# Spreading the counts of a routing search on VectorE instead of TensorE

## The chip, the cores and the metric

The kernel runs on one core of a Trainium2 chip. The metric is device time in microseconds of one execution, as the median over runs. The core has five engines with a queue of their own each: TensorE (PE in the profile; its weight loads are PEld), VectorE (DVE), ScalarE (ACT), GpSimd (POOL) and SyncE (SP, which only issues DMAs here). An engine works through its queue in the order of the program.

## The reference

Three stages in a row, all in float32:

```
x   = retention(q, k, v)            # 8 batches, 8 heads, 576 positions, 64 wide -> 4608 rows of 512
h   = top1_experts_with_capacity(x) # 8 experts of 512 -> 1024 -> 512, 576 rows each
out = (relu(h w_in) + alpha * min(h w_in, 0)) w_out      # 512 -> 2048 -> 512
```

The middle stage is what the change touches. The reference sorts all 4608 x 8 gate values and gives them out from the highest down: a row goes to the first expert that is offered to it and still has room, and every expert takes exactly 576 rows.

```
for idx in argsort(-logits.flatten()):
    tok, e = idx // 8, idx % 8
    if assigned[tok] < 0 and counts[e] < 576: assigned[tok] = e; counts[e] += 1
```

## The kernel before, in words

Rows lie as 36 chunks of 128 partitions. The attention part fills the gate values `Lg` (128 x 36 x 8). After that the kernel alternates eight experts with eight rounds of the second network: `expert(k)` multiplies the 576 rows of expert k (first layer: 16 groups of 12 matmuls over 288 columns; second layer: 8 groups of 24), `second(y, ...)` takes 512 of the resulting rows through the second network: for each of 16 blocks of the hidden width 12 matmuls `mm` over 512 columns (L969 to L971), clipping on VectorE (L974, L976), a copy on ScalarE (L978) and a subtraction on VectorE (L979) that split the result in two halves `hl`, and 12 matmuls into `acc` (L960), one block later than their `mm`. Left-over columns are gathered in `yl` for a last round.

Which rows expert k takes, and which expert comes next, is not sorted but searched, by `route(k)`. A routing finds, by bisection on the bits of each row's best remaining gate value, the highest value at which some expert becomes full. It runs over `STEPS`: six rounds, each with w thresholds (64, 32, 32, 32, 32, 65). In a round
- VectorE compares all 128 x 36 values with the w thresholds (`compare`, two halves, L425) into G,
- TensorE multiplies G by the one-hot choice O, chunk by chunk, which counts for each expert and threshold how many values lie above (`counts4`, 36 small matmuls in four row groups, L438),
- VectorE adds the four row groups (L517 to L520) and flags, per expert, the thresholds whose count has reached the expert's room R8 (`ind`, L521). These lie on 8 partitions, one for each expert,
- TensorE multiplies `ind` by a matrix of ones (L524), so that each of 128 partitions holds, per threshold, the number of experts that passed, and VectorE counts the thresholds that at least one passed (`n`, L528). From n come the thresholds of the next round (L471).

After six rounds VectorE picks for each expert the counts at the found threshold (`s8`, L535 to L538), puts them on a diagonal `D` (L540), and TensorE multiplies D by ones (L544) so that all partitions have them. VectorE then finds the expert that is full (`t8`) and how many rows with the same value it still needs (`need`, L556 to L563), marks the rows (L570, L573) and makes running counts along the chunks (L576, L578). TensorE multiplies these by two triangles (L583, L584), VectorE makes slot numbers, five small matmuls (L606) put the row numbers in order, GpSimd gathers the rows (L824), and `turn_x` and `place_x` turn and split them for the next expert.

`route(0)` runs ahead of the first expert and isn't part of the change. Routings 1 to 6 (`if k`) run beside the expert and the second network of the one before them. They are a generator: the main stream calls `tick()` at fixed places, each tick lets the routing emit its instructions up to the next `yield`, and so the yields set how far apart a routing's pieces stand in every engine's queue. The order is written out by hand; nothing moves instructions later. From the second expert on, `expert` gives 16 ticks: in the first layer after every second group, in the second layer after every group, each time ahead of the group's ScalarE and VectorE work (L918/L919, L942/L944). For the first expert the ticks of the first layer are listed in `TICKS`, and two more stand in the middle of groups (`MID`). `second` gives a tick after each `mm` block, ahead of its clipping, and one after each `acc` block. What is left of the generator at the end of `second` is emitted there.

A round takes four ticks (comparisons; counts; sums and flags; the matmul with ones), the sixth has one more, and the expert's counts take two.

## Time and profile before

| what | value |
|---|---|
| median of 3 runs | 1501.84 us (1501.71 to 1503.36) |
| profiled execution | 1498.49 us, span 1496.7 us |
| mean granted TensorE clock | 0.986 of full speed |
| TensorE busy (matmul) | 1437.6 us, 96% |
| TensorE weight loads | 1255.3 us, 84% |
| VectorE busy | 926.5 us, 62% |
| ScalarE busy | 396.4 us, 26% |
| GpSimd busy | 179.4 us, 12% |

A row of a group of instructions reads: line, engine, operation, what it writes <- what it reads, shapes, count | busy time in us, mean ns of one | idle time of the engine just ahead of them and what ended it. A matmul's busy time contains its way through the array, and matmuls overlap; the step from one start to the next says what one costs. A row in order of time reads: start, duration in us, then the same names, and in brackets idle time ahead of it with what ended it.

### The profile page before, as it was taken

The numbers are of one execution on the slowest core, as the hardware profiler recorded it, in microseconds if no ns is written. First come the engines' busy times: TensorE is split into PE (matmuls) and PEld (weight loads), VectorE is DVE, ScalarE is ACT, GpSimd is POOL, SyncE is SP. The second block draws the span as 40 slices with busy tenths as digits, with TensorE's granted clock in tenths as the row PEclk, the third lists the DMA queues.
The fourth block names the chain that finished last, engine by engine and source line by source line (L and its number), as shares of the span: only waits on it lengthen the run. The fifth ranks groups of instructions, "written<-read, shape, count | busy, mean of one in ns | idle before, by whom it ended". The sixth has DMA issues, their size and how long they took to land.

```text
span 1496.7 us, 25946 instructions
## 1 busy us (share of the span) xinstructions
PE 1437.6 (96%) x10556; PEld 1255.3 (84%) x10556; DVE 926.5 (62%) x2132; ACT 396.4 (26%) x740; POOL 179.4 (12%) x195
## 2 busy tenths in 40 slices
PE   9899958999999999999999999999999999999997
PEld 8888848978797889788978997898789888988886
DVE  4888878587846675668465856675666435333433
ACT  4566613222421141114111411141124112211111
POOL 3455511001100110011001100110012001000101
PEclk9999978999999999999999999999999999999999
DMA  8999814368734743464457444734576554355652
GB/s 296 361 344 346 312 58 162 127 254 270 222 114 169 246 134 141 169 220 132 141 175 225 133 156 172 221 131 145 193 213 160 191 214 166 107 183 188 219 192 83
DMA packets 97943, 287.57 MB, mean 192 GB/s; under 512 B 45984, under 2 KB 46368, under 8 KB 79392
## 3 DMA queue, kind: packets, MB, share of 16 engines
q1 hardware_dynamic: 78400, 230.12, 46.0%
q10 hardware_dynamic: 13344, 35.87, 6.2%
q0 software_dynamic: 6080, 19.93, 4.2%
q8 instruction: 83, 1.36, 0.4%
q14 instruction: 36, 0.29, 0.1%
HBM read 232.67 MB, written 44.04 MB: 185 GB/s over the span
## 4 chain that ended last, share of the span: by engine, by line
PE 59%; issue 17%; DVE 13%; ACT 7%; DMA 2%; POOL 1%; ACTq 1%; SPq 0%; POOLq 0%
PE acc L960 15%; PE mm L969 6%; PE mm L971 6%; PE mm L970 6%; PE mm L913 4%; PE acc L913 4%; DVE whl L799 3%; PE mm L932 2%; PE acc L932 2%; PE mm L934 2%; PE acc L934 2%; PE acc L933 2%; PE mm L933 2%; ACT whl L798 2%; DVE cv_r L226 2%
## 5 line engine op out<-in xcount | busy, mean ns | idle before, releaser
L960 PE MATMUL acc<-whl,hl 128*128 128x512 f32 x1608 | 388.3, 391 | 0.4 <-ACT hl L978 0.4
L960 PEld LDWEIGHTS acc<-whl,hl 128*128 128x128 f32 x1608 | 299.8, 188 | 65.3 <-issue 2.3
L978 ACT ACTIVATE hl<-tmp 128x512 fp32r<-128x512 f32 x144 | 91.0, 632 | 644.8 <-DVE tmp L976 639.5
L974 DVE TENSOR_SCALAR tmp<-mm,AL 128x512 f32<-128x512 f32 x144 | 107.7, 748 | 185.1 <-PE mm L971 184.6
L969 PE MATMUL mm<-act,whl 128*128 128x512 f32 x512 | 203.1, 397 | 3.8 <-ACT whl L798 2.3
L971 PE MATMUL mm<-act,whl 128*128 128x512 f32 x512 | 200.0, 391 | 0.3 <-DVE whl L799 0.3
L970 PE MATMUL mm<-act,whl 128*128 128x512 f32 x512 | 199.9, 391 | 0.0
L979 DVE TENSOR_TENSOR hl<-tmp,hl 128x512 fp32r<-128x512 f32 x144 | 99.7, 692 | 110.0 <-ACT hl L978 110.0
L824 POOL DMA_INDIRECT rows<-x_rows,gi x40 | 43.1, 1077 | 684.8 <-DVE ec L638 514.6
L969 PEld LDWEIGHTS mm<-act,whl 128*128 128x128 f32 x512 | 96.3, 188 | 24.3 <-ACT whl L798 2.7
L971 PEld LDWEIGHTS mm<-act,whl 128*128 128x128 f32 x512 | 96.5, 188 | 21.3 <-DVE whl L799 1.0
L799 DVE TENSOR_TENSOR whl<-raw,whl 128x1024 fp32r<-128x1024 f32 x80 | 97.8, 1224 | 24.7 <-ACT whl L798 24.4
L970 PEld LDWEIGHTS mm<-act,whl 128*128 128x128 f32 x512 | 96.5, 188 | 19.0
L913 PE MATMUL mm<-act,whl 128*128 128x288 f32 (+2 forms) x768 | 109.8, 299 | 0.7 <-ACT act L854 0.7
L913 PEld LDWEIGHTS mm<-act,whl 128*128 128x128 f32 x768 | 105.8, 192 | 1.8 <-ACT act L854 0.9
L913 PE MATMUL acc<-act,whl 128*128 128x288 f32 (+2 forms) x768 | 107.3, 297 | 0.0
L913 PEld LDWEIGHTS acc<-act,whl 128*128 128x128 f32 x768 | 103.7, 189 | 0.3
L976 DVE SCALAR_TENSOR_TENSOR tmp<-mm,tmp 128x512 f32<-128x512 f32 x144 | 99.6, 692 | 5.0
L798 ACT ACTIVATE whl<-raw 128x1024 fp32r<-128x1024 f32 x80 | 84.0, 1051 | 26.0 <-DVE eqc L642 26.0
L1003 POOL DMA_INDIRECT out<-rows,ix x32 | 34.4, 1076 | 443.4 <-DVE rows L999 438.2
L932 PE MATMUL mm<-act,whl 128*128 128x288 f32 x256 | 76.7, 300 | 0.0
L932 PE MATMUL acc<-act,whl 128*128 128x288 f32 x256 | 76.6, 299 | 0.0
(236 smaller groups left out, 2221.5 us busy)
## 6 DMA issues: line engine op xcount, KB each, us to landing
whl<-w_parts SPq DMA_DIRECT2D x128, 1024.0 KB, 4.8
raw<-in_w SPq DMA_DIRECT2D x64, 512.0 KB, 4.3
a_in<-in_att SPq DMA_DIRECT2D x34, 768.0 KB, 6.8
cv_in<-in_w SPq DMA_DIRECT2D x32, 512.0 KB, 7.8
w_parts<-whl ACTq DMA_DIRECT2D x16, 1024.0 KB, 6.2
x_rows<-xn ACTq DMA_DIRECT2D x36, 256.0 KB, 5.5
w_f<-cv_r ACTq DMA_DIRECT2D x32, 256.0 KB, 7.0
raw<-w_f SPq DMA_DIRECT2D x16, 512.0 KB, 5.8
```

Source lines behind the costliest of these rows:

```text
L798: ACT.activation(w[:, 0], t, AF.Copy)
L799: V.tensor_tensor(w[:, 1], t, w[:, 0].bitcast(F32), op=OP.subtract)
L913: PE.matmul(ps, w[:, wi, wc], x[:, xi, c, hh], start=(wi, xi, c) == (0, 0, 0), stop=(xi, c) == (1, 3))
L932: PE.matmul(ps, w[:, 0, cs], h[:, 0, c % 4, hh], start=c == 0, stop=False)
L960: PE.matmul(acc[tt], hl[:, hi, tt * 128:tt * 128 + 128], w[:, wi, 512:1024], start=f == 0 and (wi, hi) == (0, 0), stop=False)
L969: PE.matmul(ps, w[:, 0, cs], y[:, 0, c, 0:512], start=c == 0, stop=False)
L970: PE.matmul(ps, w[:, 0, cs], y[:, 1, c, 0:512], start=False, stop=False)
L971: PE.matmul(ps, w[:, 1, cs], y[:, 0, c, 0:512], start=False, stop=c == 3)
L974: V.tensor_scalar(t, ps, 0.0, AL[:, f:f + 1], op0=OP.min, op1=OP.mult)
L976: V.scalar_tensor_tensor(g, ps, 0.0, t, op0=OP.max, op1=OP.add)
L978: ACT.activation(hl[:, 0], g, AF.Copy)
L979: V.tensor_tensor(hl[:, 1], g, hl[:, 0].bitcast(F32), op=OP.subtract)
```

## The change

In routings 1 to 6 the two multiplications by ones are gone. `passed` does the first on VectorE: the flags are written to the top 8 rows of a 32-row tile of zeros (`IND[w]`, one for each of the three widths rounded up to 32), turned in blocks of 32 x 32 so that thresholds lie on partitions, the maximum over experts is taken, this is repeated over 32 columns and turned back, which puts all thresholds' answers on each of 32 partitions, and their sum is n. `spread` copies n from partitions 0 to 31 to the other three quarters. After the sixth round the chosen counts `s8`, now in the first rows of a 32-row tile, are turned in the same way (`every`), the small work on them runs on 32 partitions, and `spread` copies its two results. The yields around the removed matmuls are gone, and the first round has one more between its comparisons and its counts. A routing before has 25 yields from the first comparisons to the end of the sixth round's last matmul and two more to the running counts; after, 14 to the same point.

```diff
@@ -353,7 +353,12 @@
     slots2 = keep.tile([128, 2, 640], F16, name="slots2")
     C2 = {}
 
+    IND = {w: keep.tile([32, -(-w // 32) * 32], F32, name=f"ind{w}") for w in sorted({w for _, w in STEPS})}
+    s32 = keep.tile([32, 2], F32, name="s32")
+
     def route_consts():
+        for t in (*IND.values(), s32):
+            V.memset(t, 0.0)
         V.tensor_copy(RT[:, 36:38], CONST["pcol"])
         C2["j01"] = CONST["j01"].rearrange("p (z j) -> p z j", z=2)
         V.memset(Aw, 0.0)
@@ -438,6 +443,25 @@
             PE.matmul(GT["p"][r:r + 8, :w], O[:, c, :], GT["G"][:, c, :w], start=c < 4, stop=c >= NCH - 4,
                       tile_position=(0, r))
 
+    def spread(t):
+
+        for a in (32, 64, 96):
+            V.tensor_copy(t[a:a + 32], t[0:32])
+
+    def passed(ind):
+
+        b = ind.shape[1] // 32
+        turned = rt.tile([32, 3, 32], F32, name="turned")[:, 0:b]
+        flat = turned.rearrange("p a b -> p (a b)")
+        some = rt.tile([32, 3], F32, name="some")[:, 0:b]
+        n = small("n", 1, bufs=2)
+        V.transpose(flat, ind)
+        V.tensor_reduce(some, turned[:, :, 0:8], axis=AX.X, op=OP.max)
+        V.transpose(flat, some.unsqueeze(2).to_broadcast([32, b, 32]))
+        V.tensor_reduce(n[0:32], flat, axis=AX.X, op=OP.add)
+        spread(n)
+        return n
+
     EXP, IDX, GI = {}, {}, {}
 
     def route(k):
@@ -477,7 +501,7 @@
                         compare(key, thr, w, a, b)
                     if k:
                         yield
-                        if s == 5:
+                        if s in (0, 5):
                             yield
                     if k:
                         counts4(w)
@@ -509,7 +533,6 @@
                     u = [ua, ub]
                 yield
                 p = GT["p"]
-                ind = rt.tile([8, 65], BF, name="ind")
                 tot = p[0:8, 0:65]
                 if k:
 
@@ -518,9 +541,11 @@
                     V.tensor_tensor(tot[:, :w], p[64:72, :w], tot[:, :w], op=OP.add)
                     V.tensor_tensor(tot[:, :w], p[96:104, :w], tot[:, :w], op=OP.add)
                     V.tensor_tensor(tot[:, :w], p[0:8, :w], tot[:, :w], op=OP.add)
+                    V.tensor_scalar(IND[w][0:8, :w], tot[:, :w], R8[:, 0:1], None, op0=OP.is_ge)
+                    n = passed(IND[w])
+                    continue
+                ind = rt.tile([8, 65], BF, name="ind")
                 V.tensor_scalar(ind[:, :w], tot[:, :w], R8[:, 0:1], None, op0=OP.is_ge)
-                if k:
-                    yield
                 PE.matmul(p[:, 128:128 + w], ones8, ind[:, :w], start=True, stop=True)
                 yield
                 sj = small("sj", 65)
@@ -528,7 +553,7 @@
                 V.tensor_scalar(sj[:, :w], p[:, 128:128 + w], 0.5, 0.0, op0=OP.is_ge, op1=OP.add, accum_out=n)
 
             j01 = C2["j01"]
-            s8 = rt.tile([8, 2], F32, name="s8")
+            s8 = s32[0:8, :]
             cc = rt.tile([8, 2], F32, name="cc")
             for zi in range(2):
                 scr = rt.tile([8, 65], F32, name="scr", bufs=2)
@@ -536,12 +561,18 @@
                                        op1=OP.mult, accum_out=cc[:, zi:zi + 1])
             V.tensor_tensor(s8[:, 0:1], cc[:, 0:1], R8, op=OP.is_ge)
             V.tensor_tensor(s8[:, 1:2], R8, cc[:, 1:2], op=OP.subtract)
-            D = rt.tile([8, 2, 8], F32, name="D")
-            V.tensor_tensor(D, ident[0:8, None, 0:8].to_broadcast([8, 2, 8]),
-                            s8.unsqueeze(2).to_broadcast([8, 2, 8]), op=OP.mult)
             if k:
-                yield
-            PE.matmul(p[:, 256:272], ones8f, D.rearrange("p a b -> p (a b)"), start=True, stop=True)
+
+                every = rt.tile([32, 2, 32], F32, name="every")
+                V.transpose(every.rearrange("p a b -> p (a b)"), s32.unsqueeze(2).to_broadcast([32, 2, 32]))
+                z0, z1 = every[:, 0, 0:8], every[:, 1, 0:8]
+            else:
+                D = rt.tile([8, 2, 8], F32, name="D")
+                V.tensor_tensor(D, ident[0:8, None, 0:8].to_broadcast([8, 2, 8]),
+                                s8.unsqueeze(2).to_broadcast([8, 2, 8]), op=OP.mult)
+                PE.matmul(p[:, 256:272], ones8f, D.rearrange("p a b -> p (a b)"), start=True, stop=True)
+                z0, z1 = p[:, 256:264], p[:, 264:272]
+            h = z0.shape[0]
             T = small("T", 1)
             V.scalar_tensor_tensor(T, n, 1.0, u[1], op0=OP.mult, op1=OP.add)
             gt = small("gt")
@@ -551,16 +582,19 @@
             gv_ = small("gv_")
             V.tensor_tensor(gv_, gt, vm, op=OP.mult)
             V.tensor_tensor(Aw, Aw, gv_, op=OP.add)
-            yield
-            zc = small("zc", 8)
-            V.scalar_tensor_tensor(zc, p[:, 256:264], -100.0, ecol, op0=OP.mult, op1=OP.add)
-            zm = small("zm", 1)
+            if not k:
+                yield
+            zc = small("zc", 8)[0:h]
+            V.scalar_tensor_tensor(zc, z0, -100.0, ecol[0:h], op0=OP.mult, op1=OP.add)
+            zm = small("zm", 1)[0:h]
             V.tensor_reduce(zm, zc, axis=AX.X, op=OP.min)
-            t8 = small("t8", 1)
-            V.tensor_scalar(t8, zm, -1.0, -92.0, op0=OP.mult, op1=OP.add)
-            nd = small("nd", 8)
-            need = small("need", 1)
-            V.scalar_tensor_tensor(nd, zc, zm, p[:, 264:272], op0=OP.is_equal, op1=OP.mult, accum_out=need)
+            tn = small("tn", 2)
+            t8, need = tn[:, 0:1], tn[:, 1:2]
+            V.tensor_scalar(t8[0:h], zm, -1.0, -92.0, op0=OP.mult, op1=OP.add)
+            nd = small("nd", 8)[0:h]
+            V.scalar_tensor_tensor(nd, zc, zm, z1, op0=OP.is_equal, op1=OP.mult, accum_out=need[0:h])
+            if k:
+                spread(tn)
         ei = small("ei", 1, I32, bufs=2)
         V.tensor_scalar(ei, t8, -1.0, 8.0, op0=OP.mult, op1=OP.add)
         EXP[k] = ei
```

## Rows read from the trace of the kernel before

**Rows 1.** One second network: stretch, length, busy PE, PEld, DVE, ACT, POOL, clock
```profile
447.50:536.00 88.50, 88.50 (x497) 71.22 (x497) 56.09 (x143) 12.88 (x22) 5.45 (x6) 1.00 0.58 189
```

**Rows 2.** Groups of instructions on TensorE, 240 to 1100 us
```profile
L524 PE MATMUL misc<-ind,ones 8*128 8x32 bf16 (+2 forms) x36 | 6.8, 188 | 2.2 <-DVE ind L521 2.2
L544 PE MATMUL misc<-D,ones8f 8*128 8x16 f32 x12 | 2.3, 268 | 0.0
```

**Rows 3.** TensorE in order of time around one spreading matmul
```profile
573.24 0.29 PE L934 MATMUL acc<-act,whl 128*128 128x288 f32 x1
573.46 0.18 PE L524 MATMUL misc<-ind,ones 8*128 8x32 bf16 x1
573.58 0.40 PE L932 MATMUL acc<-act,whl 128*128 128x288 f32 x1
573.81 0.29 PE L933 MATMUL acc<-act,whl 128*128 128x288 f32 x1
573.94 0.30 PE L934 MATMUL acc<-act,whl 128*128 128x288 f32 x1
```

**Rows 4.** Waits of TensorE, 240 to 1100 us: total, times, longest
```profile
PE misc L438 <- DVE G L425: 6.0, 7, 1.1
...
PE misc L524 <- DVE ind L521: 2.2, 1, 2.2
```

**Rows 5.** Granted clock (the number behind POOL) in four stretches
```profile
262.00:265.00 3.00, 3.00 (x15) 2.77 (x13) 1.70 (x7) 0.40 (x2) 0.00 (x0) 0.63 0.55 175
...
326.60:330.00 3.40, 3.40 (x15) 2.74 (x15) 2.35 (x4) 1.58 (x2) 0.00 (x0) 1.00 0.95 345
377.00:381.00 4.00, 1.52 (x5) 0.48 (x3) 2.96 (x4) 1.57 (x2) 0.00 (x0) 0.91 0.92 258
381.00:384.00 3.00, 2.85 (x7) 2.32 (x8) 2.64 (x7) 1.15 (x2) 0.00 (x0) 0.55 0.91 339
```

**Rows 6.** TensorE in order of time, start of a second network
```profile
594.02 0.50 PE L969 MATMUL mm<-act,whl 128*128 128x512 f32 x1
...
599.69 0.18 PE L524 MATMUL misc<-ind,ones 8*128 8x32 bf16 x1
```

**Rows 7.** VectorE in order of time, 576 to 635 us
```profile
576.39 0.19 DVE L471 SCALAR_TENSOR_TENSOR thr<-n,tb 128x32 f32<-128x32 f32 x1
576.61 1.43 DVE L425 TENSOR_TENSOR G<-hf,thr 128x576 bf16<-128x576 f32 x2
...
594.85 0.18 DVE L517 COPY tot<-misc 8x32 f32<-8x32 f32 x1
...
597.08 0.75 DVE L974 TENSOR_SCALAR tmp<-mm,AL 128x512 f32<-128x512 f32 x1 [1.12 <-PE mm L971]
597.86 0.69 DVE L976 SCALAR_TENSOR_TENSOR tmp<-mm,tmp 128x512 f32<-128x512 f32 x1
599.25 0.69 DVE L979 TENSOR_TENSOR hl<-tmp,hl 128x512 fp32r<-128x512 f32 x1 [0.70 <-ACT hl L978]
...
620.58 0.22 DVE L517 COPY tot<-misc 8x65 f32<-8x65 f32 x1
...
621.61 0.25 DVE L521 TENSOR_SCALAR ind<-tot,R 8x65 bf16<-8x65 f32 x1
...
626.53 0.28 DVE L535 SCALAR_TENSOR_TENSOR scr<-tables,n,tot 8x65 f32<-8x65 f32 x1
...
627.24 0.16 DVE L540 TENSOR_TENSOR D<-c_ident,s 8x16 f32<-8x16 f32 x1
...
632.06 0.15 DVE L546 SCALAR_TENSOR_TENSOR T<-n,ub 128x1 f32<-128x1 f32 x1
...
634.00 0.21 DVE L578 TENSOR_TENSOR_SCAN sc<-tables,eqm 128x36 bf16<-128x36 f32 x1
```

**Rows 8.** Groups of instructions on VectorE: one column, and 180 columns
```profile
L508 DVE SCALAR_TENSOR_TENSOR ub<-n,ua 128x1 f32<-128x1 f32 x14 | 2.1, 151 | 0.0
...
L639 DVE TENSOR_REDUCE rf<-ec 128x5 f32<-128x180 f32 x8 | 2.7, 342 | 0.3
```

## The prediction, made blind

> **What bounds the kernel now.** I read the share of busy time by engine first, and then only the stretches that the change touches: the six background routings, 240 to 1100 us. In one whole run of the second network (88.5 us) TensorE is busy all the time, VectorE for 56.1 us of it and ScalarE for 12.9 [rows 1]. The reader should see two things there: whatever TensorE no longer does is time won, and VectorE is free for a third of the time on average, which says nothing yet about a single stretch. The second view was TensorE's groups of instructions: 36 spreading matmuls (six routings of six rounds) and 12 for the chosen expert's counts (six pairs) [rows 2]. Then TensorE in order of time around one of these, its waits, and VectorE in order of time around a routing's end.
>
> **What goes.** A spreading matmul costs more than its 188 ns of busy time suggests. In the first layer the step from the start of the last large matmul to that of the next one, past the small one, is 573.24 to 573.58 = 0.34 us, where an undisturbed step is 0.13; the step after it is 0.23 too [rows 3]. So 0.21 + 0.10 = 0.31 us each, 36 x 0.31 = 11.2 us. The pair for the expert's counts has two matmuls of 268 ns instead of one of 188 [rows 2]; I take 0.5 us for each of six, 3.0 us (between 0.31 and 0.62, one and two such interruptions). Waits go as well: in the stretch TensorE waits 6.0 us for the comparisons and 2.2 us, once, for the flags [rows 4]. The flags' wait goes with its matmul. The comparisons' waits nearly all belong to the first round, whose counts are put off by one more tick, that is by 24 matmuls or 3.1 us, against a longest wait of 1.1 us. Together 8.2 us. Behind the two such waits of the first background routing the granted clock is 0.63 for 3 us [rows 5]: 3 x 0.37 = 1.1 us more. Sum of what goes: 23.5 us.
>
> **What comes on VectorE, and where.** A round used four ticks and now uses two, so the routing needs 13 ticks fewer. An expert from the second on gives 16 ticks (8 in each of its two layers). By count, the sixth round's counts then fall on tick 16, the end of the expert; everything from the sum of the four parts to the two running counts is tick 17, behind the first 12 matmuls of the second network; and the matmuls with the triangles are tick 18, behind the next 12. Tick 17 is one unbroken block on VectorE, and the clipping of the first 512 columns (L974, L976, L979) stands behind it in program order.
>
> Its length, from starts in [rows 7]: sums 620.58 to 621.61 = 1.03, flag 0.28; the two sums for the expert and its flags 626.53 to 627.24 = 0.71; threshold to running counts 632.06 to 634.21 = 2.15. New and not shown anywhere are three turns of blocks, two reductions and six copies to other partitions. Their bounds are one column at 0.151 us and 180 columns at 0.343 [rows 8]; for 32 to 96 columns I take 0.22 to 0.25 a turn, 0.19 and 0.25 a reduction, and for the copies, which don't wait for each other, 0.11 to 0.19: together 1.9 us, between 1.4 and 2.9. Block: 1.03 + 0.28 + 0.71 + 2.15 + 1.9 = 6.1 us (5.6 to 7.1). The Trainium skill (VectorE: DVE Perf Modes, section "The three transpose paths") gives 311 ns for VectorE's turn of a 128x128 bf16 block; no run here shows one yet, and at that price for each of the three turns the block would be 6.3 us and the whole sum 1 us more.
>
> Now the path. After an expert the second network's matmuls start at 594.02, and TensorE comes to tick 18 at 599.69 [rows 6]. VectorE is done with the expert's last columns at 594.85 and does only 1.1 us of routing before it waits for the first 12 matmuls, until 597.08 [rows 7]. In the changed kernel the block runs from 594.85 to 600.95. So the triangle matmuls hold TensorE for 1.3 us. The clipping can only begin then; from its start to the time when the first half for the next matmul is ready is 597.08 to 599.25 = 2.2 us. So the first matmuls into `acc` start at 603.1 instead of 599.8: 3.3 us lost, for each of the five routings that run beside the experts 1 to 5 (0-based): 16.5 us (13.5 to 21.5 with the block's bounds). Later blocks of that network don't lose again, since the lead of one block of 512 columns is restored.
>
> The other rounds. Sums and flag (1.1 us at 32 columns), spreading (1.2), next threshold and two comparisons (576.39 to 578.04 = 1.65 [rows 7]) make a block of 4.0 us in one tick. The counts of two rounds are 48 matmuls of 0.13 us and the first counts' 0.4 apart, 6.7 us, and VectorE gets to the block only some 3 us after the first counts (a group of 12, ScalarE's pass and VectorE's own). 3.05 + 4.0 = 7.05: about 0.3 us of wait, of which the half of the comparisons that is used later hides some. I take 0.75 us for the rounds of a routing, 3.8 us for five; below it nothing, if VectorE is at hand earlier, and above it 1.5 each.
>
> The routing beside the first expert is a case of its own, as three of its ticks follow each single group of 12 matmuls, about 1.6 us apart. First round: its counts come only 1.4 us later than now, 1.0 us of wait stays. Second round: 3.7 us between the counts where VectorE needs about 6.5: 2.8 us. Sixth round: comparisons over 65 columns (2.7 us) and two ticks in the middle of groups: 1.7 us. Its last block stands before the subtraction that ends the expert's output, and the second network's first matmuls want that after 2.1 us: 3.2 us. Together 8.7, of which I keep 8.
>
> The clock. A gap in which TensorE was busy for 1.52 of 4 us was followed by 3 us at a mean granted clock of 0.55, the half-speed level for most of it, so 1.35 us lost; a single wait of 2.2 us ending at 326.6 was followed by full clock [rows 5]. The new gap of 3.3 us, with two tiny matmuls inside, lies between; I count half of 1.35 for each of six, 4 us (0 to 8).
>
> Moved without cost, I think: five gathers on GpSimd's queue, ten transposing DMAs and one read of the expert's number on SyncE's, all some 13 ticks (36 us) earlier. On SyncE they then stand between loads of the second network's weights that are issued two pieces ahead, about 11 us; that cover would have to be lost before a load is late. The four clears fall in the attention part, beside TensorE. Building the next expert's input also moves off the end of the second network; there I count neither gain nor loss, and up to 4 us either way in the range.
>
> **Sum.** 16.5 + 3.8 + 8 + 4 = 32.3 us come, 23.5 go: +9 us. The profiled execution took 1498.49 us, 3.35 less than the median of the runs, 1501.84. So 1507.5 in its terms, and 1511 against the median.
>
> **Rivals.**
> The other side: the last block is the only new wait. VectorE, busy for two thirds of the time [rows 1], reaches the rounds' blocks in time, the clock stays up as after 326.6, and the first expert's routing costs 3 us. 16.5 + 3 - 23.5 = -4: 1498 us. It decides at whether VectorE's wait for ScalarE within the experts is long enough to hide 4 us blocks; for it, it idles a good deal there; against it, that idle time is in pieces in front of single instructions that it can't pass.
> Cover everywhere: no new wait, all 23.5 won, 1478 us. This needs the last block to be under 2.8 us, where its rows that exist already come to 4.2. I hold little of it.
> VectorE becomes the bound in more places: the block at 7.1 us (21.5), rounds at 1.5 each (7.5), 12 for the first routing, the clock down after every gap (8), less 23.5: +26, 1527 us. For it speaks that turning and building the next input lands in the busy middle of the second network, and that delays on VectorE add up in one queue.
>
> **Chances.** Forecast 0.50, only the last block 0.24, cover 0.08, VectorE bound 0.18. A run of this kernel tells a change from none at about 0.2%, 3 us. The second case straddles that: 0.15 of its 0.24 faster. Faster 0.15 + 0.08 + 0.02 = 0.25, within 0.2% 0.13, slower 0.62. The range leaves out the full cover and the upper part of the last case: 1495 to 1526. Within the forecast alone it is 1504 to 1519.
>
> **What would show it.** Right: no matmul from flags is left; the counts' block starts two ticks after the one before; at the start of each second network the triangle matmuls wait 1 to 2 us for the running counts (L578 of the kernel before) and the first matmuls into `acc` wait about 2 us for ScalarE's half (L978), five times; the granted clock dips there. Wrong: the triangle matmuls wait for nothing, or the block on VectorE is under 4 us; then the second case or the cover holds. If waits by comparisons rise above 10 us in total, or loads of weights are waited for, it is the last one.

## The result, and the profile after

The changed kernel takes 1519.92 us (median of 6 runs, 1515.35 to 1522.33) against 1502.17 us (6 runs, 1499.1 to 1503.37) of the kernel before beside it: a ratio of 1.0119 (95% interval 1.0101 to 1.0137), 17.75 us slower. The direction was forecast and the time lies within the range, but the forecast was +9 us. The profiled execution of after took 1522.33 us, at the upper end of its runs, that of before 1498.49, just below the six runs here. The two profiles therefore differ by 23.8 us, and the account below, which is made from them, explains that difference and not the 17.75.

First the page of after, its shares by engine. TensorE's busy time is unchanged within 0.2 us (1437.6 before) although 48 matmuls are gone; VectorE has 40 us more.

```profile
PE 1437.8 (95%) x10508; PEld 1264.7 (83%) x10508; DVE 966.7 (64%) x2334; ACT 398.8 (26%) x740; POOL 174.9 (12%) x195
```

Then TensorE's waits over the six background routings, 240 to 1130 us (what waited, on what; total us, times, longest). They answer to [rows 4].

```profile
PE acc L994 <- ACT hl L1012: 14.6, 10, 2.8
PE misc L443 <- DVE G L430: 9.6, 16, 2.7
PE misc L617 <- DVE sc L612: 7.9, 5, 1.6
PE mm L1003 <- DMA whl<-w_parts: 2.7, 5, 0.7
```

The first and the third row are the two waits that were forecast at the start of each second network: the triangle matmuls (L617) for the running counts (L612), and the first matmuls into `acc` (L994) for ScalarE's half (L1012). Of the first row, 5.5 us lie in the first routing (five waits) and 9.1 us, 1.8 each, in the five others. The second row, the waits for comparisons, is 6.6 us in the first routing. The wait for flags is gone with its matmul. The fourth row is new: second networks wait for their weights.

The place itself, TensorE in order of time (start, duration, line, ..., idle time ahead and its releaser), where [rows 6] had the same stretch of another network:

```profile
757.72 0.39 PE L1005 MATMUL mm<-act,whl 128*128 128x512 f32 x1
759.67 0.16 PE L617 MATMUL misc<-sc,tri 128*128 128x2 bf16 x1 [1.57 <-DVE sc L612]
759.70 0.16 PE L618 MATMUL misc<-sc,trii 128*128 128x2 bf16 x1
761.70 0.79 PE L994 MATMUL acc<-whl,hl 128*128 128x512 f32 x1 [1.84 <-ACT hl L1012]
```

From the start at 757.72 to that at 761.70 pass 3.98 us with two tiny matmuls inside. An undisturbed step would be 0.23. The first matmul behind it takes 0.79 us instead of 0.39: it runs at half the clock. How long that lasts is in the windows (stretch, length, busy time of PE, PEld, DVE, ACT, POOL, then the granted clock, DMA share, GB/s), which answer to [rows 5]:

```profile
752.00:757.00 5.00, 5.00 (x57) 4.18 (x57) 3.98 (x22) 0.47 (x2) 0.00 (x0) 1.00 0.58 210
757.00:762.00 5.00, 1.59 (x8) 1.05 (x7) 4.04 (x20) 0.63 (x1) 0.00 (x0) 0.91 0.01 2
762.00:767.00 5.00, 5.00 (x13) 3.84 (x13) 4.20 (x11) 0.63 (x1) 0.00 (x0) 0.50 0.00 0
767.00:775.00 8.00, 8.00 (x39) 6.42 (x38) 4.03 (x12) 0.63 (x1) 0.21 (x1) 0.94 0.45 162
```

TensorE is busy from 762 to 767 and yet has 13 matmuls in these 5 us, where 5 us at the full clock (752 to 757) hold 57 with small counts among them, or 23 to 24 of this size alone. 0.50 is the lower of its two levels, 1.2 of 2.4 GHz. With the 0.91 and the 0.94 beside it, the lower level holds for about 7 us. By the clock alone 5 x 0.50 + 8 x 0.06 = 3.0 us are lost here.

Now VectorE in the same stretch: the last block, in order of time. It answers to [rows 7].

```profile
753.15 0.22 DVE L540 COPY tot<-misc 8x65 f32<-8x65 f32 x1
...
754.18 0.24 DVE L544 TENSOR_SCALAR ind<-tot,R 8x65 f32<-8x65 f32 x1
754.46 0.27 DVE L458 STREAM_TRANSPOSE turned<-ind 32x96 f32<-32x96 f32 x1
754.76 0.17 DVE L459 TENSOR_REDUCE some<-turned 32x3 f32<-32x24 f32 x1
754.96 0.27 DVE L460 STREAM_TRANSPOSE turned<-some 32x96 f32<-32x96 f32 x1
755.26 0.24 DVE L461 TENSOR_REDUCE n<-turned 32x1 f32<-32x96 f32 x1
755.53 0.46 DVE L449 COPY n<-n 32x1 f32<-32x1 f32 x3
...
756.72 0.23 DVE L567 STREAM_TRANSPOSE every<-s 32x64 f32<-32x64 f32 x1
...
758.35 0.51 DVE L449 COPY tn<-tn 32x2 f32<-32x2 f32 x3
...
759.41 0.21 DVE L612 TENSOR_TENSOR_SCAN sc<-tables,eqm 128x36 bf16<-128x36 f32 x1
759.54 0.72 DVE L1008 TENSOR_SCALAR tmp<-mm,AL 128x512 f32<-128x512 f32 x1
```

From 753.15 to 759.54 it is 6.4 us without a pause (6.1 forecast), and the clipping (L1008) stands right behind it, as worked out. The new instructions: three turns 0.27, 0.27 and 0.23 us, two reductions 0.17 and 0.24, six copies 0.46 + 0.51, together 2.15 us (1.9 forecast, 1.4 to 2.9).

**Account.** The first expert of the background part starts at 233.8 us before and 235.0 after, the second at 394.4 and 398.7, the seventh at 1121.9 and 1146.0 (first matmuls of each first layer); from there on nothing changes. So 1.2 us lie ahead of all of this, the first background routing costs 3.1 us, and five others 19.8, or 4.0 each.

For one of these five, on average:
- the gap at the last block: 3.4 (the 3.98 less its regular step and the 0.33 of two small matmuls),
- the half clock: 2.35 (about 2.9 in three of the networks, where the mean granted clock of the 8 us around the slow matmuls is 0.57 or 0.58, and 1.4 in the other two, where it is 0.79 and the lower level lasts half as long),
- the rounds: 1.0 (36 counts lie in a step of 0.56 when nothing waits; in the second round's it is 1.18, in the third's 0.93),
- waits for weights: 0.5 (2.7 in all).

In all 7.3. What goes is 3.3: 6 x 0.31 for the spreading matmuls, 0.5 for the pair, and 0.9 of waits at the first round's counts (a step of 1.72 before and 0.59 now, 1.13 less, in four of the five; the one beside the second expert had no such wait before, its step was 0.60). 7.3 - 3.3 = 4.0.

### The profile page after: what moved, and what is told of

It is laid out like the page before. It is cut to its first block, busy times and chain, and to the rows that moved or that the text cites. A ratio compares the mean times of both kernels' runs of the same rounds, so it can differ in the third digit from the quotient of the medians.

```text
span 1520.6 us, 26052 instructions
## 1 busy us (share of the span) xinstructions
PE 1437.8 (95%) x10508; PEld 1264.7 (83%) x10508; DVE 966.7 (64%) x2334; ACT 398.8 (26%) x740; POOL 174.9 (12%) x195
## 4 chain that ended last, share of the span: by engine, by line
PE 58%; issue 17%; DVE 14%; ACT 6%; DMA 3%; SPq 1%; POOL 1%; ACTq 0%; POOLq 0%
PE acc L994 16%; PE mm L1003 5%; PE mm L1004 5%; PE mm L1005 5%; PE mm L947 5%; PE acc L947 4%; DMA whl<-w_parts 2%; PE acc L966 2%; PE acc L968 2%; PE acc L967 2%; PE mm L966 2%; DVE cv_r L226 2%; PE mm L968 2%; PE mm L967 1%; DVE G L430 1%
## 5 line engine op out<-in xcount | busy, mean ns | idle before, releaser
L994 PE MATMUL acc<-whl,hl 128*128 128x512 f32 x1608 | 396.6, 397 | 14.6 <-ACT hl L1012 14.6
L994 PEld LDWEIGHTS acc<-whl,hl 128*128 128x128 f32 x1608 | 307.8, 192 | 81.4 <-ACT hl L1012 16.9
L1012 ACT ACTIVATE hl<-tmp 128x512 fp32r<-128x512 f32 x144 | 91.0, 632 | 637.1 <-DVE tmp L1010 635.3
L1008 DVE TENSOR_SCALAR tmp<-mm,AL 128x512 f32<-128x512 f32 x144 | 107.8, 748 | 210.3 <-PE mm L1005 209.5
```

The costliest lines, as they stand in the source:

```text
L994: PE.matmul(acc[tt], hl[:, hi, tt * 128:tt * 128 + 128], w[:, wi, 512:1024], start=f == 0 and (wi, hi) == (0, 0), stop=False)
L1008: V.tensor_scalar(t, ps, 0.0, AL[:, f:f + 1], op0=OP.min, op1=OP.mult)
L1012: ACT.activation(hl[:, 0], g, AF.Copy)
```

## The experiments

Ratios are to the kernel before, run beside each, in five rounds; its medians were 1501 to 1502 us. In the code, k counts routings and s rounds.

**The clock alone.** *fill* puts small matmuls that nobody reads into the two waits at the last block, which keep TensorE at work and leave everything else as it is.

```
+        spare = (7, 8) if 2 <= k < 7 else (0, 0)
+        for _ in range(spare[0]):
+            PE.matmul(q[:, 264:392], ident, ident, start=True, stop=True)
         PE.matmul(q[:, 0:ns], tri, sc2[:, 0:ns, NCH - 1], start=True, stop=True)
         PE.matmul(q[:, 2:2 + ns], trii, sc2[:, 0:ns, NCH - 1], start=True, stop=True)
+        for _ in range(spare[1]):
+            PE.matmul(q[:, 264:392], ident, ident, start=True, stop=True)
```

> The changed kernel, with 7 matmuls of a 128x128 constant by itself ahead of the triangle matmuls and 8 behind them, in routings 2 to 6; their result is used nowhere. At full clock they take about 1.5 and 1.8 us, less than the waits of 1.7 and 2.0 us that stand there, so VectorE's order and the waits' ends stay as they are. Theory (the clock): the 3.7 us gap is what lowers the granted clock to half behind it; with TensorE kept busy the clock stays at 1.00 there and each routing's second network is 1.4 to 3 us shorter, 8 to 12 us in all: 6 to 10 us slower than before instead of 18. Rival (moved transfers and one queue on VectorE): the time beyond the forecast comes from loads that are late and from VectorE, the clock has no part in it; no gain, 18 us slower than before or up to 3 us worse.

Measured 1509.98 us, 1.0061 (1.0044 to 1.0078): 9.9 us less than after in the medians, 8.7 by the two ratios. The windows of *fill* around the same block (its start is 5.9 us earlier):

```profile
751.50:756.50 5.00, 5.00 (x39) 4.48 (x38) 4.07 (x20) 0.63 (x1) 0.00 (x0) 1.00 0.01 2
756.50:761.50 5.00, 5.00 (x24) 4.12 (x23) 4.20 (x12) 0.63 (x1) 0.00 (x0) 1.00 0.28 85
```

The gap itself is still there. From the last matmul ahead of it to the first into `acc` pass 3.99 us, as in after:

```profile
751.84 0.39 PE L1010 MATMUL mm<-act,whl 128*128 128x512 f32 x1
...
755.83 2.34 PE L999 MATMUL acc<-whl,hl 128*128 128x512 f32 x9
```

But the clock stays at 1.00 behind the block, with 24 matmuls in 5 us where after had 13. Only what came behind the gap is gone. In the profiles the five experts with their second networks are 1.6, 2.7, 3.1, 3.0 and 1.3 us shorter than in after, 11.7 together, which is the 5 x 2.35 of the account. So about 10 us of the loss are the clock.

**The moved transfers.** *late* puts 13 empty ticks ahead of the gathers, so that gathers, transposing DMAs and the read of the expert's number stand about where they were.

```
             yield from route(k + 1)
+            for _ in range(13 if k < 6 else 0):
+                yield
```

> The changed kernel, with 13 empty ticks between the end of routings 1 to 6 and their gathers, so that gathers, transposing DMAs and the building of the next input stand where they stood before the change; all of the routing itself is unchanged. Theory (the clock): this touches only the short waits for weight loads in the middle of the second network, 0.6 to 0.9 us each, 3 to 4 us in all, and the clock dips stay: 14 us slower than before. Rival (moved transfers): most of what was not forecast, 9 us, goes away: 9 us slower than before, and the first routing's second network changes too.

Measured 1518.2 us, 1.0107 (1.009 to 1.0125). No row of waits by a load of weights is left in its trace between 240 and 1130 us. The dips of the clock stay behind four of the five blocks. Behind the third expert's there is none, though the gap is the same 4.0 us and TensorE works 3.58 of the 7 us from 605 in both kernels. The 8 us behind that, first in after and then in *late*:

```profile
612.00:620.00 8.00, 8.00 (x24) 6.30 (x25) 4.97 (x14) 0.63 (x1) 0.00 (x0) 0.64 0.20 59
612.00:620.00 8.00, 8.00 (x35) 6.63 (x36) 6.51 (x16) 1.21 (x2) 0.00 (x0) 1.00 0.37 133
```

This expert with its second network takes 1.0 us more than before in *late*, and 4.2 in after. In the medians *late* takes only 1.7 us less than after; in the profiled executions (1518.2 and 1522.33) it is 4.1, most of it this missing dip. What tells better how a load comes to be late is SyncE's queue in after (SPq: instructions that issue DMAs, start and duration):

```profile
784.19 0.32 SPq L829 DMA_DIRECT2D whl<-w_parts  x1
784.56 13.98 SPq L895 DMA_TRANSPOSE xt<-rows  x6
798.64 0.53 SPq L829 DMA_DIRECT2D whl<-w_parts  x1
801.48 5.41 SPq L895 DMA_TRANSPOSE xt<-rows  x4
806.93 4.78 SPq L829 DMA_DIRECT2D whl<-w_parts  x4
```

Six transposing DMAs hold the queue for 14 us. They fill `xt` in pairs, and `xt` has two buffers, so the third pair waits until VectorE has read the first (L870), for 4.6 us; the rest is mostly the issuing, some 1.3 us each. The next load of weights stands behind them, at 798.64. The first of the group issued from 806.93, behind four more transposes, lands at 812.00; TensorE waits for it until 812.05.

**The length of the last block.** *split* cuts it with two yields.

```
                     n = passed(IND[w])
+                    if s == 5:
+                        yield
                     continue
...
-            if not k:
-                yield
+            yield
```

> The changed kernel, with two more yields in the last block of routings 1 to 6: after the number of passed thresholds of the sixth round, and after the rows above the threshold have been marked. The block of 6.4 us becomes three of 2.7, 1.9 and 2.0 us with the clipping of the second network between them; nothing else moves but what follows, by two ticks. Theory (last block, and the clock behind it): the triangle matmuls wait for nothing, the first matmuls into acc wait under 0.7 us, no clock dip; 5 x 3.7 + 10 = 27 us less than the changed kernel in routings 2 to 6, and a little less in the first: 7 to 10 us faster than before. Rival (VectorE as a whole is too full in these stretches): the waits only move to the next blocks, and at most half of it comes back: 4 to 10 us slower than before.

Measured 1503.5 us, 1.0008 (0.9999 to 1.0018): 16 us less than after, but not below the kernel before. In its profile the clock falls behind none of the five blocks (1.00 from 400 to 1128 us). Its waits, in the same view and stretch:

```profile
PE misc L618 <- DVE sc L613: 7.2, 6, 1.3
PE mm L1004 <- DMA whl<-w_parts: 3.9, 5, 1.4
PE acc L995 <- ACT hl L1013: 3.7, 6, 1.1
```

The wait for ScalarE's half has fallen from 14.6 to 3.7 us. The triangle matmuls still come one piece of VectorE's work too early, and the loads are waited for longer, so the two ticks by which the transfers move are not what brings the gain.

**A cheaper way to the same gain?** *yield0* is the kernel before with one more yield, between the first round's comparisons and counts, as the change has it.

```
-                        if s == 5:
+                        if s in (0, 5):
                             yield
```

> The kernel before, with one more yield between the first round's comparisons and its counts, which is the part of the change that does not move work to VectorE. Theory: the waits of the counts for the first comparisons (four of 1.15 us, 2.3 us in the first routing and the clock dip behind them) go: 5 to 8 us faster than before. Rival: the routing ends one tick later and the next input is built later, so that the first expert's second network gives it back: no change.

Measured 1502.77 us, 1.0009 (0.9998 to 1.002): no gain, against 5 to 8 us expected. The waits tell why:

```profile
PE mm L913 <- ACT act L874: 7.2, 10, 2.1
```

The waits for comparisons fall from 6.0 us to 2.4, but the whole routing is a tick later, and the next expert's first matmuls (L913) now wait for the input that ScalarE places (L874). The kernel before has no tick to spare; the change, with 13 fewer, can pay for it.

**The first background routing.** *first_old* leaves routing 1 as before (`if k > 1` for `if k`).

```
-            if k:
+            if k > 1:
                 spread(tn)
...
```

The other branches of the routing are changed in the same way, with their yields.

> The changed kernel, with the routing beside the first expert done as before the change (matmuls with ones, four ticks a round) and the other five as changed. Theory (the first routing's ticks are too close together for its blocks): in the profile of the changed kernel the first expert and its second network take 4.3 us more than before, and that comes back: 14 us slower than before. Rival (the first routing is neutral as in the forecast, about 1 us, the rest was the executions' spread): 17 to 18 us slower.

Measured 1518.28 us, 1.0105 (1.0089 to 1.0122): 1.6 us less than after in the medians, 4.1 in the profiled executions. The sign is as expected, the size can't be told from the medians.

**More room.** *compact* cuts the last block in three and takes back one tick in the sixth round. *roomy* also gives each round a tick.

```
-                        if s in (0, 5):
+                        if s == 0:
                             yield
...
                     n = passed(IND[w])
+                    if s == 5:
+                        yield
...
-            if not k:
+            yield
+            if k:
                 yield
...
+        if 0 < k < 7:
+            yield
         ns = 2 if k < 7 else 1
```

and *roomy*, written against *compact*:

```
                         yield
-                        if s == 0:
-                            yield
+                        yield
...
-                    if s == 5:
+                    if s >= 4:
                         yield
```

> The changed kernel with the last block cut in three as in the run with two more yields, one empty tick between second and third piece and one ahead of the triangle matmuls, and the sixth round's counts one tick earlier, so that the first piece falls where VectorE waits for the expert's last group. The rounds before the sixth are as changed. Theory: with both waits at the second network's start gone no clock dip is left either; against the run with two yields (1.8 us slower than before) the wait of 1.4 us at the triangle matmuls goes five times: 5 to 6 us faster than before. Rival (VectorE is too full there): the third piece delays the clipping again, no faster than before.

> The changed kernel with as many ticks as before the change may take: one empty tick between the comparisons and the counts of each round, the fifth round's and the last block cut in pieces as above, empty ticks around them. VectorE does the spreading, TensorE only counts, as in the change. Theory: what the change removes from TensorE, 12 to 14 us, and the first comparisons' waits, 4.7 us, are won, and no block is waited for: 12 to 17 us faster than before. Rival (the forecast's third case, VectorE as a whole is too full): waits appear at other places, less than 5 us faster.

Measured: *compact* 1503.08 us, 1.0007 (0.9992 to 1.0023), and *roomy* 1517.54 us, 1.0103 (1.0087 to 1.0119), both expected well under the kernel before. In both no triangle matmul waits any more in routings 2 to 6, and the gap is gone. What takes the gain back is not the same in the two. In *compact*, the first routing's stretch (230 to 410 us):

```profile
PE misc L443 <- DVE G L430: 8.1, 6, 3.2
PE acc L999 <- ACT hl L1017: 7.8, 4, 4.4
```

and the five others (410 to 1140 us):

```profile
PE mm L1008 <- DMA whl<-w_parts: 7.2, 5, 1.9
PE misc L443 <- DVE G L430: 2.9, 10, 0.4
```

and in *roomy*, in those five:

```profile
PE mm L1007 <- DMA whl<-w_parts: 18.9, 8, 3.6
```

The profiled execution of *compact* took 1509.0 us, the longest of its twelve (from 1495.48). In it the first expert with its second network takes 10.4 us more than before (after: 3.1), at a mean granted clock of 0.93 (0.97 in after and before), while the five others together take 4.2 us less than before in spite of their loads. In *roomy* it is the other way round: the first takes 2.7 us more, the five others 12.0. The waits for weights were 2.7 us in after; at these ticks they are 7.2 and 18.9. Here my theory, that the block's length and the clock are all that stands between the change and its gain, fell short: the block was cured, the time stayed, and the first routing and the loads became the suspects.

**The second half undone.** *counts_pe* brings back the diagonal and its matmul with ones for the chosen counts, with the yields around it.

```
-            if k:
-                every = rt.tile([32, 2, 32], F32, name="every")
-                V.transpose(every..., s32...to_broadcast([32, 2, 32]))
-                z0, z1 = every[:, 0, 0:8], every[:, 1, 0:8]
-            else:
+            if True:
                 D = rt.tile([8, 2, 8], F32, name="D")
...
+                if k:
+                    yield
                 PE.matmul(p[:, 256:272], ones8f, ...)
```

> The changed kernel with its second half undone: the chosen expert's counts go through the diagonal and the matmul with ones again, with the yields around them, and the number of passed thresholds stays on VectorE. Theory (the length of the block ahead of the clipping costs, whatever is in it): the block is cut at 3.6 us, the first matmuls into acc wait 0.8 us instead of 2.0 and the triangle matmuls 1 us instead of 1.7, no dip: 1 to 4 us slower than before. Rival (the turned spreading in the rounds is what costs): still over 10 us slower.

Measured 1501.88 us, 0.9996 (0.9982 to 1.001), 18 us less than after. With one more multiplication by ones in each routing it does better, since its yields stand in the block, and no gap is left there (a step of 0.30 us from the last matmul ahead to the first into `acc`, 3.98 in after). Its waits for weights are longer than in after, 5.4 us. So the length in one piece is what costs, not the work.

**The forecast's own terms.** *blocks_only* puts *fill*, *first_old* and *late* (for routings 2 to 6) together. What is left is what the forecast had for those five routings without the clock: last blocks and rounds, less what goes. In code, only the ticks, which begin one routing later than in *late*:

```
+            for _ in range(13 if 1 <= k < 6 else 0):
+                yield
```

> The changed kernel with what was not forecast taken out: the first routing as before, TensorE kept busy by matmuls of a constant in the two waits of routings 2 to 6, and 13 empty ticks ahead of their gathers. What is left is what the forecast counted for these five routings: 11.8 + 4.7 us won by the removed matmuls and the first comparisons' waits, against 17.2 us for the last blocks and 6.2 us for the rounds' waits. Theory: +7 us, 5 to 9 us slower than before. Rival (something else still costs): 12 us slower or more.

Measured 1506.66 us, 1.0042 (1.0027 to 1.0058): +6.3 us by the ratio, 4.1 to 8.7. In its profile the five experts with their second networks take 2.1, 1.0, 1.0, 0.9 and 1.0 us more than before, 6.0 together; the first is the one that had no wait at the first round's counts to win. With what the account has for gap and rounds, less what goes, it would be 3.4 + 1.0 - 3.5 = 0.9, and 2.0 for that one. So these terms add up, as a sum; no run takes one of them alone.

**Cured blocks with the first routing as before.** *compact_late* is *compact* with routing 1 as before and 9 empty ticks ahead of the gathers; *roomy_old* is *roomy* with routing 1 as before; *roomy_late* is that with 3 empty ticks. The ticks of *compact_late* (in *roomy_late* 3 in place of 9):

```
             yield from route(k + 1)
+            for _ in range(9 if 1 <= k < 6 else 0):
+                yield
```

> The compact version (last block cut in three, sixth counts one tick earlier) for routings 2 to 6, the first routing as before, and 9 empty ticks ahead of the gathers, which puts gathers and transposing DMAs where they were before. Theory (transposes that wait on SyncE's queue hold up the loads of the second network's weights behind them): the compact version's waits for weights, 1.3 to 2.0 us each, go, and its first routing's loss of 10 us; 8 to 13 us faster than before. Rival (the waits for weights come from memory traffic, wherever the gathers stand): 2 to 4 us faster at most.

> The roomy version (an empty tick in each round, blocks cut) for routings 2 to 6, the first routing as before. Its gathers stand three ticks earlier than before the change. Theory: the waits for weights of 3.4 to 4 us and the clock dips behind them stay, five times, the first routing's 10 us go: 2 to 8 us slower than before. Rival (the first routing was all of it): 10 us or more faster than before.

> As the run before it, with 3 empty ticks ahead of the gathers of routings 2 to 6, so that they stand where they were before the change. Nothing else differs. Theory (the place of the transposes among the weight loads on SyncE's queue): all waits for weights go; what is left is what the change removes from TensorE and the first comparisons' waits, 12 + 4.7 us: 13 to 20 us faster than before. Rival (VectorE too full, memory traffic): less than 5 us faster.

Measured 1508.32 us, 1.0037 (1.0023 to 1.0051); 1511.5 us, 1.0065 (1.0045 to 1.0085); 1498.92 us, 0.9981 (0.9967 to 0.9994). Three misses, and all on the side of the loads: the waits for weights are 12.6, 19.5 and 11.5 us in the three. The trace of *roomy_late* shows how it comes about. TensorE waits for one load at 528.88:

```profile
528.88 0.50 PE L1013 MATMUL mm<-act,whl 128*128 128x512 f32 x1 [2.15 <-DMA whl<-w_parts]
```

and SyncE's queue ahead of that:

```profile
507.72 0.32 SPq L839 DMA_DIRECT2D whl<-w_parts  x1
508.09 13.98 SPq L905 DMA_TRANSPOSE xt<-rows  x6
...
522.80 0.37 SPq L839 DMA_DIRECT2D whl<-w_parts  x1
```

The kernel before has the same work in this order:

```profile
511.26 2.78 SPq L861 DMA_TRANSPOSE xt<-rows  x2
...
514.77 0.37 SPq L795 DMA_DIRECT2D whl<-w_parts  x1
515.23 16.13 SPq L861 DMA_TRANSPOSE xt<-rows  x6
```

It is the same, fourteenth load of this second network, which starts at 448.29 there and at 448.83 here. Before, it is issued at 514.77, between the first two transposes and the other six. With the gathers one tick earlier it stands behind six, at 522.80, 8.0 us later, and lands at 528.83, just ahead of the end of TensorE's wait. I had put the gathers on tick 37 of the second network's count; in the kernel before the first is on tick 38.

**One tick.** With that, three kernels that differ from three others by one empty tick: *roomy_38* (4 for 3), *compact_38* (10 for 9), and, the other way, *late12* (12 for 13 in *late*). In code, for *roomy_38*:

```
-            for _ in range(3 if 1 <= k < 6 else 0):
+            for _ in range(4 if 1 <= k < 6 else 0):
                 yield
```

> The roomy version with the first routing as before and 4 instead of 3 empty ticks ahead of the gathers of routings 2 to 6: one tick later, the same tick as in the kernel before. Theory (a load of weights issued behind a pair of transposing DMAs that waits for its buffer): the last load of the second network's weights is issued ahead of the second pair again, the five waits of 2.3 to 3.2 us and the dips behind them go: 14 us less than with 3, 15 to 18 us faster than before. Rival (memory traffic at that time, whatever the order): 3 to 6 us faster than before, as with 3.

> The compact version with the first routing as before and 10 instead of 9 empty ticks ahead of the gathers of routings 2 to 6, the same tick as in the kernel before. Theory: five waits of 2.5 to 3.3 us and the dips behind four of them go, 18 us less than with 9: 10 to 13 us faster than before; the rest against the roomy version is the rounds' waits, 5 to 6 us. Rival: no change by that tick.

> The changed kernel with 12 instead of 13 empty ticks ahead of the gathers: one tick earlier than in the kernel before. Nothing else differs. Theory: a wait for weights of about 2.5 us appears at the end of five second networks where there was none with 13, with clock dips behind some: 10 to 15 us slower than with 13, 27 to 31 us slower than before. Rival: as with 13, 16 us slower than before.

Measured:

| kernel | median us | ratio to before (95%) | against its pair |
|---|---|---|---|
| roomy_38 | 1484.0 | 0.9883 (0.9865 to 0.99) | -14.9 |
| compact_38 | 1488.2 | 0.9916 (0.9898 to 0.9934) | -20.1 |
| late12 | 1541.11 | 1.0258 (1.0233 to 1.0284) | +22.9 |

All three went the way expected (*late12* further than expected). *roomy_38* is 17 us faster than the kernel before. In its profile the five experts with routings 2 to 6 beside them take 2.6, 3.7, 3.7, 3.8 and 3.7 us less than before. TensorE's longest groups of waits over the whole stretch are then these; none is of a load, and the one for the running counts (0.6 us, once) is not among them:

```profile
PE misc L554 <- DVE ind L551: 2.4, 2, 2.2
PE misc L443 <- DVE G L430: 2.3, 3, 1.1
PE mm L1013 <- ACT whl L842: 1.7, 1, 1.7
```

and SyncE's queue has the order of before, the load at 514.78 ahead of the six:

```profile
509.71 3.31 SPq L905 DMA_TRANSPOSE xt<-rows  x2
...
514.78 0.32 SPq L839 DMA_DIRECT2D whl<-w_parts  x1
515.19 16.60 SPq L905 DMA_TRANSPOSE xt<-rows  x6
```

In *late12* the one tick brings the load behind the six (issued at 533.05, in *late* at 522.97 between two transposes and six), and the late load also brings the clock down. Windows of *late12* around such a wait (2.47 us, ending at 539.46):

```profile
534.00:539.00 5.00, 2.99 (x14) 2.13 (x12) 3.96 (x8) 1.34 (x3) 0.00 (x0) 1.00 1.07 324
539.00:544.00 5.00, 4.54 (x14) 3.66 (x15) 3.36 (x6) 1.71 (x3) 0.00 (x0) 0.66 0.87 227
```

## Why the prediction came out as it did

Point by point, forecast against the profile of after (us):

| term | forecast | measured |
|---|---|---|
| last blocks, five | 16.5 | 17 |
| rounds, five | 3.8 | 5 |
| first routing | 8, and 0.7 of the clock | about 11, if 8 went |
| clock, the other five | 3.3 | 11.8 (*fill* against after: 11.7 in the profiles, 9.9 in the medians) |
| gathers, transposes, loads of weights | 0 | 2.7 by the waits |
| what goes, five routings | 15.5 | 16.3 |
| what goes, first routing | 8 | 8, not measured apart |
| ahead of the routings | 0 | 1.2 |

The mechanism was right: the block in one piece on VectorE, the clipping behind it, the two waits and their sizes. Its length was 6.4 against 6.1 us, and the gap 3.4 against 3.3. *split*, which only cuts it, takes back 16 us; *counts_pe*, which cuts it and gives the chosen counts back to TensorE, 18. What failed is the size of one term, and a term put at nothing. That the time still lies in the range owes nothing to these two: the clock came out beyond its own bound, and the range had room from other terms. The new instructions cost about what was taken for them. (The lower bound of the last blocks, 13.5, was a slip: a block of 5.6 us gives 14.) The Trainium skill's 311 ns for a turn of a 128x128 bf16 block (VectorE: DVE Perf Modes, "The three transpose paths") is an upper figure here: the turns took 0.20 us for 32 float32 columns on 32 partitions, 0.23 for 64 and 0.27 for 96.

The first step that failed is "I count half of 1.35 for each of six, 4 us". It was taken between two rows of before: a gap in which TensorE worked 1.52 of 4 us, and one of 2.2 us without a fall [rows 5]. Here TensorE worked 1.59 of 5 us, more like the first of the two, and the lower level lasted for some 7 us in three networks and half as long in two. Even the 1.35 left out a part: the row ahead of it has 0.91 over 4 us, 0.36 us more. 2.35 us each, three and a half times the 0.68 that I took, is the larger part of what is missing. The bound "0 to 8" was too low as well.

The second is "Moved without cost, I think". The sentence behind it even names the loads on SyncE and their 11 us of cover, but it put no price on how long six transposing DMAs hold the queue, their issue and the wait for a buffer together: 14 us, more than the cover. The kernel before has such a hold too, of 16 us; there the load stands ahead of it. In after the loads cost only some 3 us, by luck of the tick; one tick made 15 to 23 us in the three pairs, clock included.

Of the rivals, the one with VectorE as the bound had the clock down after every gap and, as its sign, loads that are waited for; both came (its other sign, over 10 us of waits by comparisons, just not: 9.6), and the result lies half-way between its 1527 and the forecast. But its cause isn't what happened: the rounds of a routing cost 1.0 us and not its 1.5, and with its pieces short, the same work on VectorE is hidden. The full cover, held at 0.08 and put at 1478 us for this kernel, did not happen in it; but it is nearly what *roomy_38* shows (1484 with the first routing as before): in the five routings all that goes is won once the block is cut and the transfers are where they were.

In the first routing the waits for comparisons came where they were worked out, two of them longer: 0.9 us in the first round (1.0 forecast), 3.3 in the second (2.8) and 2.9 in the sixth (1.7), by the steps over the 36 counts (1.45, 3.85 and 3.47 us, less 0.56).

What stays open: the first routing's loss, which the medians don't resolve (1.6 us) and the profiles put at 3 to 4, and which was 10.4 in the profile of *compact*; and why a gap of the same 4.0 us is followed by a long fall of the clock, a shorter one, or, once in *late*, none. This is probably part of why executions of after differ by 7 us among themselves: the fastest, 1515.35, has the highest granted clock of the six, 0.982, and the others lie between 0.975 and 0.979.

## What to carry to other kernels

A wait on the critical engine is priced with what it does to the clock behind it: look in the windows at the stretch after the nearest gap of like busy time, not only at the gap, take it in full, and give it a wide range, since gaps of one size were not followed by one loss. When work is handed to an engine in an order written by hand, cut it into pieces no longer than the lead of what stands behind it, before judging whether the engine has time. And when a change shortens a chain, keep the transfers at its end where they were until their queue has been read: one tick earlier put a load behind transfers that waited for a buffer, and that alone moved the kernel by 15 to 23 us, about as much as the change.

## What the runs showed of the hardware

- TensorE's granted clock was 0.50 for about 7 us behind a stretch in which it worked 1.59 of 5 us, though two tiny matmuls stood in its middle and no single wait was over 1.84 us; with unread matmuls in that gap it stayed at 1.00. The same gap of 4.0 us was followed in after by a loss of about 2.9 us in three networks and 1.4 in two, and once in *late* by none. A wait of 2.15 us on a load (*roomy_late*, 1.85 of 4 us busy) was followed by 1.00, one of 2.47 us (*late12*, 2.99 of 5 us busy) by 0.66, so gaps of about that size went either way.
- Six transposing DMAs, of which the third pair waits for its buffer, held the issuing queue for 14 to 16.6 us, and the loads behind them were issued only then.
- Three copies of one column from partitions 0 to 31 to the other quarters took 0.46 us together, 0.145 each, so one after another.
